# Top-k attention with two expert layers on one core: ten instead of eight slots of the fullest expert start in the attention phase

## The chip, the cores and the metric

The kernel runs on one core of one Trainium2 chip. The metric is the device time of one execution in microseconds. Three runs of the kernel before gave 954.03, 956.29 and 954.28 us; their median is 954.28 us.

## What is computed

Three layers follow each other; every tensor is float32.

1. Attention over 4 batches, 8 heads, 576 positions and head size 64. Of each row of scores only those that reach its 32nd largest value stay; softmax, then the product with v.
2. A dense layer on the 2304 tokens (512 wide): `h = max(x@w1, x@w2, x@w3)` (768 wide), then `h @ w_out`.
3. Routing: each token goes to the expert (one of 8) with the largest logit; `relu(x @ w1[e]) @ w2[e]` (1024 wide inside), scaled by the softmax weight of that expert.

```python
logits = x @ w_gate; expert_idx = np.argmax(logits, axis=1)
...
h = np.maximum(xe @ w1[e], 0.0)
out[mask] = gate_w[mask, None] * (h @ w2[e])
```

With the inputs that the reference draws, the reference's own arithmetic routes 2122 of the 2304 tokens to one expert. In the order in which the kernel ranks its 18 tiles of 128 tokens, that expert has 1051 tokens after nine tiles, 1170 after ten and 1286 after eleven.

## The kernel before, in words

The attention is cut into 144 tiles (128 query rows of one head; the last 64 rows of two heads share one). One Python loop writes out the whole program, one step (`t`, in the code also `clock[0]`) after another. In each step it issues the stages of several tiles (scores, top-k rounds on VectorE, masking, exp, the transposed probabilities, the product with v 14 steps after the scores are worked on), and then fills TensorE with units of the later layers. The order of the instructions on every engine and queue is thus fixed when the program is written; no engine chooses.

**Jobs.** One tile of 128 tokens whose attention is done becomes a job: six `unit_h` (L355, 36 matmuls of 128 columns), two `unit_x2` (L1170 to L1172, 9 matmuls of 512 columns), `unit_gate` (L1192 to L1194) and `unit_rank` (L1236, L1237). After the rank, a row of counts (`snap`) is kept, and the tile's rows are scattered to a DRAM buffer `xs` by expert (L1257, an indirect DMA of GpSimd). The tile then counts as ranked. The last job is tile 15.

**Slots.** The expert that has most tokens after two ranked tiles is picked. A slot is 128 rows of it. `open_slots` opens slot number n as soon as n+2 tiles are ranked and the slot before is open. A slot opened before step 140, and while fewer than `NS1` slots exist, is early, otherwise late; there are at most ten (`NSL`), and late ones open only after step 160.

- An *early* slot does its first layer in two visits, one for each half of the expert's first weight matrix (1024 columns in two halves of 512). Only one half is on the chip at a time, in `W1h` (`half_piece`: four loads of 256 KB, each split into a high and a low float16 part). Each visit loads the slot's rows turned (`xTe`), runs two `unit_e1` (24 matmuls of 128 columns each, L355), and writes the relu, also in two parts, to a DRAM buffer `hs` (L1432). The halves are swapped when every begun visit is done and enough slots wait for the other half: four while the step is under 140 and fewer than `NS1` slots exist, else one. When both halves of a slot are done, its hidden rows are loaded back, 512 KB, into one of two buffers `hTe` (L1385), and four `unit_e2` (L366 to L368, six matmuls of 512 columns each) do its second layer.
- A *late* slot needs the whole first matrix `W1e`, which is loaded in steps 161 to 168. Four `unit_late` (L355, tile `W1e`) do its first layer, and its hidden rows stay on the chip (L1410, L1411) in buffers of their own (three); then come the same four `unit_e2`.

**What sets the order.** `run_units` works with credit: each step adds 1.4 (1.8 once the second matrix is on the chip, 2.0 after step 160), up to 1.2 (2.5 after step 160); units are issued while it is above zero. A `unit_h` or `unit_x2` costs 1.0, a gate 0.25, a rank 0.05, any expert unit 0.67. First come visits of early slots, then jobs, then late slots' first layers, then second layers. A new job may start 2 steps after it is made, its first `unit_x2` 3 steps after its last `unit_h`, its gate 4 steps after the second `unit_x2`, its rank 2 steps after the gate; it is ranked 2 steps after that. A visit starts 2 steps after its rows are loaded and is done 3 steps after it ran. A second layer starts 2 steps after its `hTe` load is issued, and that load is issued once fewer than two early slots hold one. At most four PSUM tiles are live.

```python
early = picked and picked + 8 < clock[0] < TSTOP and len(slots) < NS1
...
if todo[half[0]]:
    ...
elif all(len(s.begun) == len(s.done) for s in slots if not s.late) and len(todo[1 - half[0]]) >= (NSWAP if clock[0] < TSTOP and len(slots) < NS1 else 1):
    half[0] = 1 - half[0]
```

In the program before, slots 0 to 7 are early and open in steps 59, 62, 67, 78, 88, 98, 105 and 110; tile 8 is the tenth ranked tile (step 122) and tile 9 the eleventh (step 129). Visits: half 0 for slots 0 to 3, half 1 for slots 0 to 7 (the last in step 120), a swap in step 123, and half 0 for slots 4 to 7 in steps 136, 139, 142 and 145. Slots 8 and 9 are late: their first layers are the units of steps 170 and 172. The last job is made in step 160; its two `unit_x2` are issued in step 167, its gate in 171, its rank in 173. Second layers: slots 0 to 5 before that rank, slots 6 to 9 behind it.

**The last stage.** `load_ahead` loads the raw weights of a second expert (eight loads of 512 KB, L1347, steps 168 to 175). When all 18 tiles are ranked, `finale` writes the last stage: zero rows behind each expert's rows in `xs` (L340, on the queues of SyncE and ScalarE), a table of what is left to do (some 60 small VectorE instructions, L268 to L331), then loads of weights (L439, L448) and rows (L423 to L428). Then seven dense tiles of the fullest expert (weights `W1e`) alternate with seven half tiles of the others.

Names in the profile: `mm<-xTe,W1h` is a first layer of an early slot, `mm<-xTe,W1e` of a late one, `mm<-…,hTe` a second layer, `ph<-W1h,W1e` the first layer of a dense tile of the last stage (its rows lie in `W1h`), and L1237 the second matmul of a rank.

Of the kernel before, what the change touches and what calls it, by code (L numbers as in the profile page):

```python
# [19 lines left out]
def kernel(  # L20
# [35 lines left out]
    DOWN = 2.0 ** -68  # L56
    LOW = -1.0e30
    UNIT_RATE, TAIL_RATE = 1.08, 2.0
    NEARLY, NPICK, NMIX, NS1 = 10, 2, 7, 8
    CAP, XA, NSL, NLD, NAHEAD = 1.2, 3, 10, 4, 4  # L60
    NSWAP, XLAG, KLAG, TSTOP, EARLY_RATE, LATE_RATE = 4, 2, 2, 140, 1.4, 1.8
    RANK_LAG = 1
# [1695 lines left out]
```

## Time and profile before

| | us |
|---|---|
| median of three runs | 954.28 |
| the profiled execution | 951.46 |
| its span, first to last instruction | 949.7 |
| TensorE busy | 751.6 |
| VectorE busy | 762.5 |
| ScalarE busy | 694.3 |
| GpSimd busy | 608.6 |
| mean granted TensorE clock, share of full speed | 0.96 |

The profile shows one execution; the time of that execution is 1.76 us longer than its span and 2.82 us under the median of the three runs. Busy shares are means over stages. In the fortieths of the span VectorE stands at 9 tenths or more through nearly all of the first 27 (some 640 us), TensorE from about there to nearly the end.

### The profile page before, as it was taken

The page shows a single profiled execution, that of the slowest core. Times are in us where ns is not written, and L with a number is a line of the kernel's source. Part 1 is how long each engine was busy: PE and PEld are TensorE (multiplying, and loading weights), DVE is VectorE, ACT ScalarE, POOL GpSimd, SP SyncE. Part 2 cuts the span into 40 slices and gives each one's busy share as a digit, 9 for nine tenths or more (in the row PEclk, how much of TensorE's full clock was granted, in tenths as well). Part 3 has the DMA queues.
Part 4 walks back from the last instruction along what each step waited for, and adds up shares of the span by engine and source line. Part 5 has one row for each costly group of instructions (what it writes and reads, how often), then busy time and mean ns, then how long its engine had stood idle before and what let it go on. Part 6 is the DMA issues. An engine that isn't in the chain of part 4 may idle for free. (4 is left out here: it accounts for less than half of the span.)

```text
span 949.7 us, 29065 instructions
## 1 busy us (share of the span) xinstructions
PE 751.6 (79%) x10606; PEld 578.1 (61%) x10606; DVE 762.5 (80%) x3110; ACT 694.3 (73%) x1463; POOL 608.6 (64%) x552
## 2 busy tenths in 40 slices
PE   0212368888777899878898998889999999999992
PEld 0100237666555677657677787567887767588881
DVE  4999999999998999998998899788972335567671
ACT  2668899997898988898897997887863231466661
POOL 1457798998988789787877898687985221111110
PEclk9999999999998999899989999889999999999996
DMA  9681977775996788699969888687799358699270
GB/s 229 204 260 29 223 158 153 138 143 105 184 165 151 143 161 175 111 206 176 173 128 179 170 139 154 131 188 127 170 168 156 91 150 278 177 299 279 63 216 16
DMA packets 372164, 155.93 MB, mean 164 GB/s; under 512 B 331931, under 2 KB 348319, under 8 KB 372000
## 3 DMA queue, kind: packets, MB, share of 16 engines
q1 hardware_dynamic: 368128, 143.10, 71.9%
q0 software_dynamic: 3136, 9.46, 2.8%
q8 instruction: 87, 1.43, 0.6%
q10 hardware_dynamic: 736, 1.32, 0.5%
q14 instruction: 77, 0.63, 0.3%
HBM read 76.06 MB, written 16.67 MB: 98 GB/s over the span
## 5 line engine op out<-in xcount | busy, mean ns | idle before, releaser
L355 PEld LDWEIGHTS <-W 128*128 128x128 f16 x4560 | 248.2, 100 | 28.0 <-issue 25.2
L965 POOL TENSOR_TENSOR f<-s,g 128x576 f32<-128x576 f32 x144 | 200.9, 1395 | 69.6 <-DVE vec L974 32.9
L355 PE MATMUL mm<-xT,W 128*128 128x128 f16 x3456 | 210.5, 222 | 18.2 <-DVE W1h L741 6.8
L1058 POOL TENSOR_TENSOR phl<-e,phl 128x576 f16<-128x576 f32 x144 | 186.3, 1293 | 8.1 <-ACT phl L1054 7.9
L913 DVE MAX8 c<-s 128x8 f32<-128x96 f32 x864 | 175.2, 243 | 8.3 <-ACT s L899 4.7
L892 PEld LDWEIGHTS <-qT 128*128 128x128 f16 (+1 forms) x640 | 56.3, 108 | 188.9 <-issue 156.6
L892 PE MATMUL S<-kt,qT 128*128 128x64 f16 (+3 forms) x320 | 62.4, 345 | 109.9 <-ACT s L899 94.4
L1077 PE MATMUL av<-vh,pt 128*128 128x65 f16 (+3 forms) x1600 | 112.4, 201 | 17.4 <-DVE xn L1126 12.9
L1043 ACT ACTIVATE e<-s,be 128x576 f32<-128x576 f32 x144 | 110.6, 768 | 7.7 <-POOL phl L1058 5.7
L974 DVE MAX8 vec<-f 128x8 f32<-128x576 f32 x144 | 108.8, 755 | 5.3 <-POOL f L965 1.4
L959 ACT ACTIVATE g<-s,bf 128x576 uint16<-128x576 f32 x144 | 111.1, 771 | 0.1
L1048 DVE SCALAR_TENSOR_TENSOR e<-s,hkth,e 128x576 f32<-128x576 f32 x72 | 104.1, 1446 | 8.3 <-ACT e L1043 8.1
L1077 PEld LDWEIGHTS <-pt 128*128 128x128 f16 (+3 forms) x2400 | 90.8, 104 | 30.5 <-issue 17.6
L1054 ACT ACTIVATE phl<-e 128x576 f16<-128x576 f32 x144 | 97.4, 676 | 11.3 <-DMA pt<-phl 11.3
L899 ACT ACTIVATE s<-S 128x576 f32<-128x576 f32 x144 | 92.3, 641 | 15.5 <-PE S L892 14.6
L1077 PE MATMUL av<-vl,pt 128*128 128x64 f16 (+3 forms) x800 | 101.6, 199 | 0.0
L1037 POOL TENSOR_TENSOR s<-s,g 128x576 f32<-128x576 f32 x72 | 95.9, 1331 | 0.3
L456 DVE SCALAR_TENSOR_TENSOR W<-st,W 128x1024 f16<-128x1024 f32 x56 | 65.8, 1220 | 36.7 <-ACT W L455 34.6
L892 PE MATMUL S<-kT,qT 128*128 128x512 f16 (+3 forms) x320 | 48.5, 293 | 18.7 <-ACT s L899 18.7
L455 ACT ACTIVATE W<-st 128x1024 f16<-128x1024 f32 x56 | 55.6, 1046 | 1.8 <-DMA st<-in_moe_w_dram 1.8
L1034 ACT ACTIVATE g<-s,hkth 128x576 uint16<-128x576 f32 x72 | 55.4, 769 | 0.0
L1161 POOL TENSOR_TENSOR hhl<-a,hhl 128x384 f16<-128x384 f32 x36 | 34.7, 964 | 28.9 <-ACT hhl L1160 28.9
(232 smaller groups left out, 1586.4 us busy)
## 6 DMA issues: line engine op xcount, KB each, us to landing
st<-in_moe_w_dram SPq DMA_DIRECT2D x72, 512.0 KB
st<-in_moe_w_dram SPq DMA_DIRECT2D x28, 256.0 KB
raw<-in_moe_w_dram SPq DMA_DIRECT2D x12, 512.0 KB
st<-in_v_dram SPq DMA_DIRECT2D x16, 256.0 KB
hs<-he SPq DMA_DIRECT2D x16, 256.0 KB
hTe<-hs SPq DMA_DIRECT2D x8, 512.0 KB
st<-in_q_dram SPq DMA_DIRECT2D x15, 256.0 KB
qT<-qT SPq DMA_DIRECT2D x30, 128.0 KB
```

The costliest lines, as they stand in the source:

```text
L355: nc.tensor.matmul(out=ps[:, o * n:(o + 1) * n], lhsT=w(b, kk, c), rhs=x(a, kk), start=(kk == 0 and i == 0), stop=(kk == KD - 1 and i == 2))
L892: nc.tensor.matmul(out=ps[o:o + m, j, 0:(REM if j else NQ * P)], lhsT=qt[:, vv, hh, 0:m], rhs=kr[:, hh] if j else km[:, hh // HG, :, hh % HG],
L913: nc.vector.max(out=c[:, i * 8:(i + 1) * 8], in_=s[:, i * CW:(i + 1) * CW])
L959: nc.scalar.activation(out=gg[n], in_=Ss[n], func=ACTF.Sign, bias=bf[g][:, i], accum_out=cnt[g][:, i])
L965: nc.gpsimd.tensor_tensor(out=ff[n], in0=Ss[n], in1=gg.pop(n).bitcast(F16), op=ALU.subtract)
L974: bulk.append(lambda: nc.vector.max(out=y8[g][:, i, 1:9], in_=y))
L1037: nc.gpsimd.tensor_tensor(out=Ss[n], in0=Ss[n], in1=zz.pop(n).bitcast(F16), op=ALU.subtract)
L1043: nc.scalar.activation(out=e, in_=Ss.pop(n) if early(n) else Ss[n], func=ACTF.Exp, scale=ESC, bias=be[g][:, i])
L1048: nc.vector.scalar_tensor_tensor(out=e, in0=Ss.pop(n), scalar=kth[g][:, i:i + 1], in1=e, op0=ALU.is_ge, op1=ALU.mult)
L1054: nc.scalar.activation(out=ph[:, 0, 0:S], in_=p, func=ACTF.Copy)
L1058: nc.gpsimd.tensor_tensor(out=ph[:, 1, 0:S], in0=p, in1=ph[:, 0, 0:S], op=ALU.subtract)
L1077: nc.tensor.matmul(out=av[o:o + m, i, 0:n], lhsT=t[0:kk, p * NCH + c, o:o + m], rhs=v_rows(x, b, c, hh)[:, 0:n], start=(c == 0 and p == 0 ...
```

## The change

One constant: `NS1`, the number of slots that may be early, goes from 8 to 10.

```diff
-    NEARLY, NPICK, NMIX, NS1 = 10, 2, 7, 8
+    NEARLY, NPICK, NMIX, NS1 = 10, 2, 7, 10
```

So the ninth and the tenth slot (8 and 9) open when ten and eleven tiles are ranked, and their first layers are done in two visits each, with the half weights, as those of the other eight. No late slot is left. The total of ten slots, their rows, and the last stage's tiles stay as they are.

## Rows read from the trace of the kernel before

**Rows 1.** The page, busy time of engines: busy us, share of span, instructions.

```profile
PE 751.6 (79%) x10606; PEld 578.1 (61%) x10606; DVE 762.5 (80%) x3110; ACT 694.3 (73%) x1463; POOL 608.6 (64%) x552
```

**Rows 2.** Stretches: us, busy of PE, PEld, DVE, ACT, POOL; clock, DMA share, GB/s.

```profile
700.00:760.00 60.00, 59.74 (x812) 45.46 (x809) 22.03 (x86) 21.19 (x41) 28.63 (x34) 1.00 0.65 126
760.00:800.00 40.00, 39.87 (x442) 27.92 (x439) 14.91 (x56) 12.28 (x25) 7.16 (x9) 1.00 0.66 196
...
796.40:817.30 20.90, 20.86 (x100) 9.38 (x98) 15.18 (x72) 6.91 (x9) 3.13 (x4) 1.00 0.73 267
817.30:819.40 2.10, 0.07 (x2) 0.07 (x2) 2.10 (x3) 2.10 (x3) 1.62 (x1) 1.00 0.63 125
819.40:935.70 116.30, 113.29 (x1848) 91.20 (x1847) 72.40 (x79) 67.84 (x86) 14.21 (x15) 1.00 0.71 194
```

**Rows 3.** Groups by line, whole span: first layers of early, then late slots.

```profile
L355 PE MATMUL mm<-xTe,W1h 128*128 128x128 f16 x768 | 48.5, 224 | 1.1 <-DVE xr L1178 0.8 <-DMA xTe<-xs 0.3
...
L355 PE MATMUL mm<-xTe,W1e 128*128 128x128 f16 x192 | 11.1, 219 | 0.1
```

**Rows 4.** Timeline of TensorE, 785 to 825 us: start, us, what, idle before.

```profile
785.02 5.52 PE L355 MATMUL mm<-xTe,W1e 128*128 128x128 f16 x96
...
790.96 5.53 PE L355 MATMUL mm<-xTe,W1e 128*128 128x128 f16 x96
...
796.36 0.17 PE L1237 MATMUL mm<-oh,ones 128*128 128x8 f16 x1
...
816.88 0.38 PE L368 MATMUL mm<-vh,hTe 128*128 128x512 f16 x1
819.33 5.52 PE L355 MATMUL ph<-W1h,W1e 128*128 128x128 f16 x96 [2.06 <-DMA W1h<-xs]
```

**Rows 5.** Groups of TensorE from 796.4 to 817.3 us; one of six alike.

```profile
L366 PE MATMUL mm<-kt,hTe 128*128 128x512 f16 x16 | 6.1, 379 | 0.0
```

**Rows 6.** Timeline of VectorE behind the last rank.

```profile
796.57 0.17 DVE L1264 TENSOR_TENSOR vec<-mm,base 128x8 f32<-128x8 f32 x1 [1.34 <-PE mm L1237]
...
797.16 0.69 DVE L1411 SCALAR_TENSOR_TENSOR hTe<-mm,hTe 128x512 f16<-128x512 f32 x1
...
809.27 0.18 DVE L331 TENSOR_TENSOR chg<-new,live 1x31 int32<-1x31 f32 x1
```

**Rows 7.** Timelines of GpSimd (first row) and of SyncE's queue, same stretch.

```profile
798.98 0.99 POOL L1257 DMA_INDIRECT xs<-xr,si  x1 [9.74 <-DVE lv L270]
...
805.36 4.40 SPq L340 DMA_DIRECT2D xs<-zrow  x4
812.18 1.26 SPq L439 DMA_DIRECT2D st<-in_moe_w_dram  x4
...
816.14 1.30 SPq L427 DMA_TRANSPOSE W1h<-xs  x1
```

**Rows 8.** DMAs: loads of hidden rows, SyncE's wait for their buffer (700 to 800 us), all scatters.

```profile
hTe<-hs SPq DMA_DIRECT2D x8, 512.0 KB
...
SPq L1385 <- PE mm L368: 7.7, 2, 6.0
...
DMA to landing us min/median/max: 3.3/4.3/6.3
```

**Rows 9.** Stretches as in rows 2: a TensorE gap, then three times 3 us.

```profile
378.90:383.50 4.60, 0.04 (x1) 0.00 (x0) 4.50 (x7) 0.70 (x3) 3.12 (x4) 0.82 0.41 91
383.59:386.59 3.00, 3.00 (x22) 1.67 (x22) 2.93 (x19) 2.51 (x6) 1.16 (x1) 0.50 0.02 5
386.59:389.59 3.00, 3.00 (x14) 1.15 (x12) 2.88 (x18) 3.00 (x7) 1.65 (x3) 0.65 0.49 90
389.59:392.59 3.00, 3.00 (x61) 2.89 (x60) 2.94 (x15) 3.00 (x9) 2.89 (x3) 1.00 0.86 194
```

**Rows 10.** Splitting of half weights on VectorE, whole span, and a gap of 1.7 us.

```profile
L741 DVE TENSOR_TENSOR W1h<-mm,W1h 128x512 f16<-128x512 f32 x11 | 7.6, 691 | 10.9 <-ACT mm L740 10.7
...
697.66 0.18 PE L1236 MATMUL mm<-oh,tri 128*128 128x8 f16 x1 [1.70 <-DVE oh L1226]
```

## The prediction

> **What bounds the kernel now.** The busy times of the engines come first: TensorE and VectorE are both near 80% [rows 1], so the stage decides. The stretches of the end show which: from 700 us on TensorE is busy 59.74 of 60 us and then 39.87 of 40 at clock 1.00, while VectorE stands at 22.03 of 60 and 14.91 of 40 [rows 2]. The last stage, 819.4 to 935.7 us, is TensorE's too (113.29 of 116.3). The order of TensorE's work shows the joint: the first layers of slots 8 and 9 run at 785.0 and 791.0 us, the last rank ends at 796.5, then second layers run until 817.26, then TensorE is idle for 2.06 us until the last stage's rows have landed at 819.33 [rows 4]. So two things compete to set when the last stage starts: the work that TensorE still has, and the chain behind the last rank. The chain wins by 2.06 us today. Its links: the rank's counts on VectorE, the scatter issued at 798.98, the zero rows issued at 805.36 when it has landed, the table done at 809.45, weight loads at 812.18, the load of rows at 816.14 [rows 6, 7]. From rank to first matmul it takes 819.33 - 796.36 = 23.0 us.
>
> **What the change moves.** Slots 8 and 9 open at ten and eleven ranked tiles, steps 122 and 129, both under 140. The tokens of the expert are then 1170 and 1286, over the 1152 and 1280 that nine and ten full slots need, so both are full and the last stage's list stays the same. The swap in step 123 comes as before: slot 8 is not open yet, and four slots wait. Half 0 then serves slots 4 to 9: the new visits run in steps 148 and 151, right behind slot 7's in 145. In step 154 the halves are swapped a third time (after step 140 one waiting slot is enough), the four pieces of half 1 are loaded again in 155 to 158, and the other visits run in 163 and 166.
>
> *First layers on TensorE.* Removed: 192 matmuls, 11.1 us [rows 3]. Added: 192 of the same form; at the mean of the early ones, 48.5/768 x 192, they take 12.1 us, but that mean holds stretches of low clock, and here the clock is 1.00 [rows 2]. I take 11.4, so +0.3 (bounds 0 and +1.0). Old and new place lie in the same solid stretch: steps 148 to 166 are about 703 to 770 us, and TensorE idles 0.26 us between 700 and 760. **Nothing is saved by the move itself.**
>
> *The order.* This is the term that counts. Following the credits by hand: the visit in 148 delays tile 12's second `unit_x2` to 149, the one in 151 sends slot 1's second layer to 153 and 159 (before: 151, 152) and slot 2's to 160, 166, 167. The two visits after 160 go ahead of the jobs, so the last `unit_h` of tile 15 slips from step 164 to 165, its `unit_x2` from 167 to 168, its gate from 171 to 172 and its rank from 173 to 174. Before, the late slots' units filled steps 170 and 172 and kept second layers out (in 171 three PSUM tiles were taken). Now second layers fill them: slot 4 in 170, slot 5 in 172, three units of slot 6 in 173. So 27 second-layer units stand ahead of the last rank where 24 stood, and 13 behind it where 16 stood. Sixteen take 817.26 - 796.38 = 20.9 us [rows 4]; their matmuls are 96, six groups of 16 [rows 5]; one unit is 1.3 us. All first layers are ahead of the rank in both programs. Hence the rank comes 3 x 1.3 = **3.9 us later** on TensorE, and only 13 x 1.3 = 17 us of work are left to cover its chain. If my count is off by a step, the shift is 0 or about 8 us; these are its bounds.
>
> *The chain.* One instruction goes out of it: the 0.69 us split of slot 9's hidden rows at 797.16, L1411 [rows 6]: -0.6. An earlier scatter gains little: it took 6.4 us where the median is 4.3 [rows 7, 8], but the table ends only 0.3 us before the zero rows are issued (809.45 against 809.76), so -0.3 is the bound. New ahead of it on SyncE's queue: the loads of the hidden rows of slots 8 and 9, which wait for a buffer that the second layer two slots earlier frees. The last of them waits for the end of slot 7, 1.3 + 5.2 = 6.5 us behind the rank; the zero rows waited until 8.9 us behind it (805.36 - 796.5), so it is hidden; without that cover it costs what slot 7 is late. ScalarE's half of the zero rows stands behind slot 7's output in the same way, with about 1.7 us of cover left.
>
> *The clock.* TensorE's idle time ahead of the last stage grows to 2.1 + 3.9 - 0.6 = 5.4 us. The gap of 2.07 us today and one of 1.7 us leave the clock at 1.00 [rows 2, 10]. A gap of 4.6 us does not: the next 3 us run at 0.50, the 1.2 GHz level, the 3 us after them at 0.65, then 1.00 [rows 9]. Lost are 0.50 x 3 + 0.35 x 3 = 2.5 us of full speed work, here in a stage that TensorE bounds. Bounds 0 and 2.6; I take 2.5, the gap being nearer to that row.
>
> *What costs nothing.* The half weights again: four splits of 0.69 us on VectorE [rows 10] and eight copies of 0.6 on ScalarE, in a stretch where both are idle for over half the time [rows 2]. DMA: 1 MB of weights, 1 MB out to `hs`, 1 MB back, at a DMA share of 0.65. The loads of hidden rows pace the second layers, as only two buffers serve slots 4 to 9: one is free when a slot ends, and TensorE has the next slot, 5.2 us, to cover the load. 512 KB [rows 8] at the 267 GB/s of the densest stretch [rows 2] take 2.0 us, and a load of rows needed 1.9 us from the end of its issue to its use (819.33 - 817.44), so 3.9 us are hidden in 5.2. With one raw weight load ahead of it, 5.9 us: 0.7 us shows for each of the two slots ahead of the rank. Bounds 0 and 4; I take 0, since SyncE waited for such a buffer for 7.7 us in all and TensorE never waited for a load [rows 8, 2].
>
> **The sum**: +0.3 + 3.9 - 0.6 + 2.5 = +6.1 us. Against the profiled execution, 951.46 us, that is 957.6; the median of the runs lies 2.82 us above that execution, so **960.4 us**, +0.6%. About 0.3%, 2.9 us, is what a measurement can tell from no change.
>
> **Rivals.**
>
> *Faster: TensorE has room.* The weight loads of TensorE, PEld, are busy 45.46 of 60 us and 27.92 of 40 [rows 2], so 26.6 us look free between 700 and 800 us, more than the 11.1 us that move. If the visits ran in that room, the rank and the work behind it would come 11.1 us earlier: 943.2 us. It decides if TensorE is truly idle where the visits are put. Against it: 96 matmuls of 512 columns in 20.9 us are 0.217 us each, and 512 columns at 2.4 GHz are 0.213; with 512 columns per load of weights a low PEld is no room. Idle time that could be filled is 0.4 us in the hundred, and the 1.7 and 2.06 us gaps [rows 10, 4], at most about 4 us (950). I give it 0.06. The Trainium skill, Perfetto Trace Analysis, section Identifying the Most-Contended Engine, says that matmul busy time is no good measure and that headroom is judged by the busy share of weight loads and by the floating-point rate; by the first the move would pay, and the rows here speak for the second.
>
> *The same.* No second layer gets ahead of the rank, because a load or a PSUM tile holds slot 6 back: +0.3 - 0.6, 954 us. Or one or two units do and the gap stays short enough for the full clock: 1.3 x 2 - 0.3 = +2.3, 956.6. For it: the margin is one step of a plan counted by hand. I give it 0.24.
>
> *Slower still: loads of hidden rows show.* Eight raw loads share SyncE's queue with them and each waits behind a buffer; if the two slots ahead of the rank and the zero rows each slip 1 to 2 us, 3 to 5 us are added: 964. Chance 0.11.
>
> *It does not do what it says.* If the count were under 1280 at step 129, a slot would be blank and its 128 rows would go to the end: a dense tile there is 5.5 + 4 x 1.3 = 10.7 us, with serial loads before it, 966 or more. The margin is 6 tokens. Chance 0.02.
>
> **The numbers.** Forecast 0.57. Slower by over 0.3%: 0.57 + 0.11 + 0.02 = 0.70; the same 0.24; faster 0.06. The range goes from 952.5, which takes in most of the same, to 966, the loads that show; within the likeliest case alone, the clock's cost at 0 and a little of the loads give 957.9 (960.4 - 2.5) to 963.
>
> **What would show it.** Right: late first layers (`mm<-xTe,W1e`) gone, 16 rows of half-weight splits, a last rank near 800 us (796.4 + 3.9 + 0.3), 13 units behind it, some 5 us of idle TensorE waiting for the rows of `W1h`, and a clock near 0.5 right after. The last stage starts near 823 us (819.3 + 3.9 + 0.3 - 0.6) and takes 2 to 3 us longer than 116.3. Wrong: a rank at 796 or earlier, no longer gap, or waits of TensorE on `hTe`; and a last stage that starts before 817 us would refute the reading that TensorE has no room.

## The result, and the profile after

Four runs of the changed kernel gave 965.0 to 970.81 us, median 968.21; four of the kernel before on the same chip gave a median of 954.15. The ratio is **1.0133** (95% interval 1.0095 to 1.0171): slower by about 13 us (14 by the medians), where +6 was forecast. The sign is right, the size is not, and 968.21 lies above the range (966.0). The profiled execution took 965.0 us. Executions over 1.5% above the fastest of their kernel are left out of the figures of this document; that is one, of 980.49 us, in the second measurement of the changed kernel.

The first layers moved as described. The group of early first layers has 960 matmuls instead of 768 [rows 3], the late form is gone, and the group costs 59.3 - 48.5 = 10.8 us more where 11.1 went. The group of the changed kernel, then its list of DMAs (28 loads of 256 KB and 8 of hidden rows stood there before):

```profile
L355 PE MATMUL mm<-xTe,W1h 128*128 128x128 f16 x960 | 59.3, 222 | 1.6 <-DVE xr L1178 0.8 <-DMA xTe<-xs 0.7
```

```profile
st<-in_moe_w_dram SPq DMA_DIRECT2D x32, 256.0 KB
...
hTe<-hs SPq DMA_DIRECT2D x10, 512.0 KB
```

The joint to the last stage looks different from [rows 4]. Timeline of TensorE of the changed kernel:

```profile
799.20 0.17 PE L1237 MATMUL mm<-oh,ones 128*128 128x8 f16 x1
...
814.70 0.38 PE L368 MATMUL mm<-vh,hTe 128*128 128x512 f16 x1
826.56 0.61 PE L366 MATMUL mm<-kt,hTe 128*128 128x512 f16 x1 [11.48 <-DMA hTe<-hs]
...
833.79 0.89 PE L355 MATMUL ph<-W1h,W1e 128*128 128x128 f16 x13
```

The rank comes at 799.2 instead of 796.4, but the last stage starts at 833.8 instead of 819.3: from the start of the rank to the stage it takes 34.6 us instead of 23.0. In between TensorE runs the second layers of slots 6, 7 and 8, then stands for 11.48 us, and what it waits for is not the rows of the last stage but the hidden rows of slot 9. The stretches say what that does to the clock (columns as in [rows 2]):

```profile
700.00:760.00 60.00, 58.60 (x843) 46.33 (x841) 23.66 (x73) 24.81 (x49) 27.97 (x33) 1.00 0.73 152
...
815.00:826.50 11.50, 0.07 (x1) 0.00 (x0) 5.32 (x5) 7.67 (x9) 2.03 (x2) 0.74 0.78 247
826.50:829.50 3.00, 2.94 (x7) 1.04 (x8) 3.00 (x4) 1.27 (x2) 0.00 (x0) 0.50 0.71 124
829.50:832.50 3.00, 3.00 (x12) 1.23 (x11) 0.85 (x1) 0.00 (x0) 0.00 (x0) 0.79 0.38 66
...
833.80:950.00 116.20, 113.36 (x1849) 91.27 (x1847) 69.19 (x76) 66.73 (x84) 15.87 (x15) 1.00 0.73 188
```

Slot 9's 24 matmuls take from 826.56 to the end of the last one at 833.96, 7.4 us, where a slot took 20.9 / 4 = 5.2 [rows 4]: 2.2 us are the clock's, at 0.50 and then 0.79. The last stage itself then runs at 1.00 and is no longer than before.

Why slot 9's hidden rows are late stands in SyncE's queue. Its timeline in the changed kernel:

```profile
793.89 0.33 SPq L1385 DMA_DIRECT2D hTe<-hs  x1
...
804.75 0.34 SPq L1385 DMA_DIRECT2D hTe<-hs  x1
...
813.24 4.36 SPq L340 DMA_DIRECT2D xs<-zrow  x4
819.97 1.26 SPq L439 DMA_DIRECT2D st<-in_moe_w_dram  x4
821.51 1.18 SPq L448 DMA_DIRECT2D st<-in_moe_w_dram  x4
822.79 0.34 SPq L1385 DMA_DIRECT2D hTe<-hs  x1
823.88 1.30 SPq L427 DMA_TRANSPOSE W1h<-xs  x1
```

The load at 793.89 is slot 6's, the one at 804.75 slot 8's. Slot 9's is issued at 822.79, behind the four issues of zero rows and eight weight loads of the last stage; its buffer had been free since slot 7 ended, about 810. And the zero rows are themselves late: at 813.24, 14.0 us behind the rank, where they were issued at 805.36, 9.0 behind it [rows 7]. They wait for the last tile's scatter, on GpSimd's queue. First the last output ahead of that scatter in the kernel before, then the changed kernel:

```profile
788.06 0.98 POOL L400 DMA_INDIRECT out_dram<-ye,mte  x1 [4.62 <-DMA out_dram<-ye,mte]
```

```profile
795.71 0.97 POOL L400 DMA_INDIRECT out_dram<-ye,mte  x1 [5.07 <-DMA out_dram<-ye,mte]
...
802.07 0.98 POOL L400 DMA_INDIRECT out_dram<-ye,mte  x1 [5.19 <-DMA out_dram<-ye,mte]
808.33 0.97 POOL L400 DMA_INDIRECT out_dram<-ye,mte  x1 [5.28 <-DVE cnt L323]
809.61 0.97 POOL L1257 DMA_INDIRECT xs<-xr,si  x1 [0.30 <-issue]
```

The scatter (L1257) was issued 2.6 us behind the rank before [rows 4, 7]; now 10.4 behind it: the outputs of slots 5 and 6 (L400, at 802.07 and 808.33) stand ahead of it in GpSimd's queue, each issued some 6.3 us after the one ahead. The rows at 795.71 and 802.07 show the wait for the output ahead to land; at 808.33 the profile names another wait, with the same spacing. Before, slot 5's output stood at 788.06, ten us ahead of the scatter, as the late slots' first layers (785 to 796 us, [rows 4]) lay between it and the rank.

### The profile page after: what moved, and what is told of

Read it like the earlier page. It is cut to its first block, busy times and chain, and to the rows that moved or that the text cites. A ratio compares the mean times of both kernels' runs of the same rounds, so it can differ in the third digit from the quotient of the medians.

```text
span 963.3 us, 29131 instructions
## 1 busy us (share of the span) xinstructions
PE 752.9 (78%) x10606; PEld 579.6 (60%) x10606; DVE 765.6 (79%) x3114; ACT 697.2 (72%) x1467; POOL 610.0 (63%) x552
## 5 line engine op out<-in xcount | busy, mean ns | idle before, releaser
L355 PEld LDWEIGHTS <-W 128*128 128x128 f16 x4560 | 252.6, 101 | 31.4 <-issue 28.5
L355 PE MATMUL mm<-xT,W 128*128 128x128 f16 x3456 | 215.0, 224 | 19.1 <-DVE W1h L741 5.9
L1077 PE MATMUL av<-vh,pt 128*128 128x65 f16 (+3 forms) x1600 | 110.3, 200 | 14.3 <-DVE xn L1126 10.3
L1048 DVE SCALAR_TENSOR_TENSOR e<-s,hkth,e 128x576 f32<-128x576 f32 x72 | 103.3, 1435 | 9.1 <-ACT e L1043 8.9
L1054 ACT ACTIVATE phl<-e 128x576 f16<-128x576 f32 x144 | 97.5, 677 | 10.4 <-DMA pt<-phl 10.4
L355 PE MATMUL mm<-xTe,W1h 128*128 128x128 f16 x960 | 59.3, 222 | 1.6 <-DVE xr L1178 0.8
L355 PEld LDWEIGHTS <-W1h 128*128 128x128 f16 x960 | 55.1, 99 | 2.9 <-issue 1.0
```

What stands on the lines that cost most here:

```text
L355: nc.tensor.matmul(out=ps[:, o * n:(o + 1) * n], lhsT=w(b, kk, c), rhs=x(a, kk), start=(kk == 0 and i == 0), stop=(kk == KD - 1 and i == 2))
L1048: nc.vector.scalar_tensor_tensor(out=e, in0=Ss.pop(n), scalar=kth[g][:, i:i + 1], in1=e, op0=ALU.is_ge, op1=ALU.mult)
L1054: nc.scalar.activation(out=ph[:, 0, 0:S], in_=p, func=ACTF.Copy)
L1077: nc.tensor.matmul(out=av[o:o + m, i, 0:n], lhsT=t[0:kk, p * NCH + c, o:o + m], rhs=v_rows(x, b, c, hh)[:, 0:n], start=(c == 0 and p == 0 ...
```

## The experiments

All ratios are to the kernel before, run on the same chip and beside it; the chip differs from group to group, so medians of different groups are not set against each other. For the reading across profiles one table is used. Its columns are worked out from timelines: the start of the 122nd tile's exponential (up to there the programs differ in little more than the place of the scatter and the opening of slot 8, some 35 us ahead of it), and from there the time to the last product with v, to the end of the last rank, to the first matmul of the last stage ("the chain" below), and to the end of the span.

| profile | 122nd tile | to last av | to rank | to stage | to end |
|---|---|---|---|---|---|
| before | 623.5 | 116.3 | 56.7 | 22.8 | 130.4 |
| before, second profile | 629.5 | 115.3 | 57.0 | 23.4 | 133.2 |
| after | 625.1 | 118.6 | 55.7 | 34.4 | 129.5 |
| after, second profile | 628.9 | 121.3 | 55.7 | 34.3 | 130.9 |
| load first | 628.8 | 119.1 | 55.7 | 29.4 | 132.4 |
| no outputs | 625.6 | 119.1 | 55.7 | 31.9 | 131.1 |
| both | 629.6 | 118.5 | 55.7 | 26.5 | 133.4 |
| before, only the traffic | 627.2 | 116.6 | 57.2 | 25.5 | 131.2 |
| nine early slots | 625.2 | 118.0 | 60.9 | 24.8 | 134.8 |
| mended, full output | 626.9 | 122.7 | 55.7 | 27.5 | 133.0 |
| mended, three buffers | 627.5 | 124.7 | 53.1 | 26.1 | 135.2 |
| before, scatter later | 608.4 | 118.0 | 57.7 | 24.6 | 133.1 |
| after, scatter later | 612.3 | 120.7 | 55.7 | 34.6 | 132.3 |
| mended, scatter later | 607.2 | 125.4 | 53.1 | 27.2 | 132.0 |

**Slot 9's load first.** The last stage's instructions are written only when every slot's load of hidden rows has been issued.

```diff
-  lambda: all(s.open for s in slots),
+  lambda: all(s.open and (s.late or s.hT is not None) for s in slots),
```

> Edit: the changed kernel, but the last stage is written only once the hidden rows of all early slots have been asked for, so slot 9's load stands ahead of the table, the zero rows and the weight loads on SyncE's queue. Theory A (that load was issued at 822.8 us instead of about 809.8, behind everything that waits for the table): the 11.5 us wait of TensorE for it goes, slot 9's second layer ends near 820, and the last stage starts when its rows land, near 826 instead of 833.8: about 960.4 us (968.2 - 7.8). Theory B (GpSimd issues the last scatter 10.2 us behind the rank instead of 2.6) is untouched by this: the zero rows stay near rank + 14. Theory C (more DMA and splitting work in the same stretch, no order): no change, 966 to 971.

966.18 us (five runs, 962.65 to 967.21), ratio 1.0085 (1.0053 to 1.0117). SyncE's queue and TensorE's only long gap near the stage, then two stretches, of this kernel:

```profile
813.95 0.34 SPq L1385 DMA_DIRECT2D hTe<-hs  x1
819.55 4.32 SPq L340 DMA_DIRECT2D xs<-zrow  x4
```

```profile
832.96 1.33 PE L355 MATMUL ph<-W1h,W1e 128*128 128x128 f16 x11 [8.68 <-DMA W1h<-xs]
```

```profile
833.00:836.00 3.00, 3.00 (x29) 3.00 (x29) 3.00 (x4) 1.70 (x2) 0.00 (x1) 0.50 0.52 137
836.00:839.00 3.00, 3.00 (x43) 3.00 (x42) 1.06 (x2) 0.60 (x1) 0.00 (x0) 0.74 0.48 88
```

The wait for hidden rows is gone and the chain is 5.0 us shorter (34.4 to 29.4): the queue order was a cause. But the chain is still 6 us longer than in the kernel before, the rows of the last stage are now what comes last, and the low clock only moves into the stage. The time came down less than to the 960 that this theory alone wants.

**No outputs of slots 5 and 6.** Their rows of the output are computed but not scattered, so this kernel leaves part of the output out.

```diff
+  if s.i in (5, 6):
+      nc.scalar.activation(out=y, in_=ps, func=ACTF.Copy, scale=mte[:, s.i, 0:1])
+  else:
+      put_y(ps, mte[:, s.i], y)
```

> Edit: the changed kernel, but the output scatters of slots 5 and 6, which stand ahead of the last tile's scatter on GpSimd's queue, are left out (those rows of the output are not written). Theory B: the last scatter is issued near rank + 3 instead of rank + 10.2, the zero rows go out some 5 us earlier, and with them the weight loads, slot 9's load and the rows; the wait of TensorE for slot 9 shrinks from 11.5 to about 7 us and the time falls by 4 to 5 us, to about 963.9. Theory A alone: slot 9's load still stands behind the table's loads, so most of the wait stays. Theory C: no change beyond 1 us.

966.7 us (965.15 to 975.57), ratio 1.0138 (1.0079 to 1.0198). GpSimd's scatter, 3.05 us behind the rank at 800.21, and TensorE's gap:

```profile
803.26 0.98 POOL L1257 DMA_INDIRECT xs<-xr,si  x1 [5.00 <-issue]
```

```profile
824.77 0.61 PE L366 MATMUL mm<-kt,hTe 128*128 128x512 f16 x1 [8.84 <-DMA hTe<-hs]
```

The scatter is back in its place and the zero rows come at 8.95 us behind the rank, as before; the chain shortens by 2.5 us only, since slot 9's load still stands behind the last stage's instructions. In the time no difference to the unedited change can be seen (1.0138 beside 1.0133).

**Both edits at once** (the output of slots 5 and 6 left out here too).

> Edit: the two edits above together. A and B together: the last stage starts near 823 us instead of 833.8, so about 957.6 us (968.2 - 10.6), 3 to 4 us over the kernel before; TensorE's gap ahead of the last stage is 2 to 4 us. If A and B each cost what they should and nothing else does, what is left against the kernel before is the rank that comes 2.8 us later. Theory C: 966 or more.

963.19 us (962.64 to 969.4), ratio 1.008 (1.0049 to 1.0111). From rank to stage 26.5 us, a gap of 5.65. So the two queues explain 34.4 - 26.5 = 7.9 of the 11.6 us by which the chain grew (34.4 - 22.8). Most of the rest seems to be the load of hidden rows itself, which now stands *ahead* of the zero rows on SyncE and waits for slot 7 until 10.7 us behind the rank, so that the zero rows go out at 11.9 instead of 9.0; that is read from the order of the queue. And 0.8% were left where the theory wanted less: the gap of 5.65 us brings the clock down in the stage (0.50 in its first 3 us, 0.69 in the next 3).

**Only the traffic.** The kernel before, with the traffic of the change and none of its work: the half weights loaded once more in steps 155 to 158, four writes to `hs` and two copies of 512 KB.

```diff
+  if not general and 155 <= t <= 158:
+      half[0] = 1
+      pend_w.append(half_piece(t - 155))
```

> Edit: the kernel before (two late slots), to which the added transport is added without its order: half 1 of the weights loaded and split once more in steps 155 to 158 (not used), four writes of 256 KB to the DRAM buffer at the steps of the new visits, and two copies of 512 KB inside DRAM at the steps of the two new loads of hidden rows. Theory C: this alone costs most of the 14 us, 962 to 968. Theories A and B: within 2 us of the kernel before, 954 to 956.

959.21 us (ten runs, 954.76 to 963.03), ratio 1.0024 (1.0001 to 1.0047): the traffic and the four splits are worth some 2 us, 4.5 at most by the interval. But the chain is 25.5 us, 2 to 3 longer than in the two profiles of the kernel before (22.8, 23.4), with a gap of 4.76 us. The zero rows go out as early as before; from them to the load of rows (L340 to L427) SyncE's queue takes 13.4 us (809.79 to 823.19) instead of 10.8 (805.36 to 816.14, [rows 7]).

**The kernel before again**, for a second profile and for the spread.

> The kernel before once more, for a second profile of it beside those of this call. In the profiles so far the attention phase ends between 739.8 and 748.1 us, which hides shifts of a few us; what is compared is the time from the last rank to the first matmul of the last stage, 23.0 us before, 34.6 after. Every theory: 23.0 within 1 us again, ratio 1.00.

957.32 us (ten runs, 954.16 to 961.8), ratio 0.9997 (0.9975 to 1.0019). Its profile is 8.7 us longer than the first, 6.0 of them at the 122nd tile: executions of one and the same kernel drift apart in the attention. The chain is the same (23.4 us).

**Nine early slots.** One constant: `NS1` is 9, so only slot 8 moves.

> Edit: NS1 = 9, so only one of the two slots moves. In this plan all loads of hidden rows stand ahead of the last stage's instructions, and the late slot 9 keeps its own buffer; 28 units of second layers stand ahead of the last rank (24 before), and the output scatters of slots 5 and 6 stand right ahead of the last tile's scatter. Theory B and the plan: no wait of TensorE for hidden rows; the last scatter is issued near rank + 6 to 10, the zero rows near rank + 12 to 14, the last stage starts 26 to 30 us behind the rank, and the rank itself is 5 us later: 960 to 965 us. If the cost simply went with the number of slots moved, it would be half of that of the changed kernel, near 961, with half of its wait for hidden rows (5 to 6 us).

966.99 us (965.01 to 969.25), ratio 1.0098 (1.0061 to 1.0134). One slot costs nearly as much as two, 2 us more than the expected 960 to 965. The chain is nearly the old one (24.8 us, where 26 to 30 were expected), with the scatter issued 3.4 us behind the rank, but here the fault that was forecast for ten slots does come: 28 units of second layers stand ahead of the rank, which comes 60.9 us behind the attention's end instead of 57, and 12 units don't cover the chain (the clock is 0.50 and 0.60 in the first two stretches of 3 us behind this gap):

```profile
828.91 1.33 PE L355 MATMUL ph<-W1h,W1e 128*128 128x128 f16 x11 [9.21 <-DMA W1h<-xs]
```

**Mended, with the full output.** Slot 9's load first, and the outputs of slots 5 and 6 kept back until the last scatter is issued.

```diff
+  put_y(ps, mte[:, s.i], y, held if clock[0] >= 173 and len(ranked) < NTT else None)
...
   ranked.append(j)
+  if len(ranked) == NTT:
+      for go in held:
+          go()
```

> Edit: the changed kernel with the last stage written only after all hidden rows are asked for, and with the output scatters of slots 5 and 6 held back until the last tile's scatter is issued (nothing left out). Theories A and B: like the run with both edits, 26 to 27 us from the last rank to the last stage, near 962; what remains over 23.0 is SyncE's queue, which holds the zero rows back behind slot 9's load, as that waits for the end of slot 7's second layer, 10.6 us behind the rank. If the left-out output itself was what saved time, it stays near 966.

967.43 us (961.33 to 972.37), ratio 1.0096 (1.006 to 1.0132), though the chain is 27.5 us. That misses the expected 962 and is no better than the version that left the outputs out. By the time alone the rival of the expectation, that the output left out was itself what saved time, is not excluded; by the chain (27.5 beside 26.5) holding the outputs back does what leaving them out does. This profile also has a long masking at 652.9 us (see below) and 122.7 us to the last product with v.

**Mended, three buffers.** Three buffers `hTe` instead of two (the load no longer waits for slot 7), the outputs held, and a bound on the second layers ahead of the rank, which gives 22 units ahead and 18 behind.

```diff
-  if sum(...) < (2 if e1 else 1):
+  if sum(...) < (3 if e1 else 1):
...
+  ahead_of = 20 if any(j.u <= NU1 + 2 for j in jobs) else 22 if jobs else 99
+  if len(slots) == NSL and 4 * s.i + s.u - 4 >= ahead_of:
+      continue
```

> Edit: the changed kernel with three buffers for hidden rows instead of two, the output scatters of slots 5 and 6 held back as above, and second layers held so that 22 units stand ahead of the last rank and 18 behind it. Theories A and B plus the queue: no load of hidden rows waits long on SyncE's queue, the zero rows go out near rank + 9, the last stage starts 23 us behind the rank and TensorE has 18 x 1.3 = 23.5 us to fill that, so no gap: 2 us less than the kernel before, ratio 0.998, and 14 to 16 us less than the changed one. Theory C (the added transport itself costs): still 5 us or more over the kernel before.

965.93 us (twelve runs, 959.46 to 969.14), ratio 1.007 (1.0041 to 1.0099). The expectation was missed. The chain is 26.1 us: the zero rows go out at 9.2 us behind the rank, as in the kernel before, but from them to the load of rows it takes 13.0 us (814.36 to 827.33) instead of 10.8, as in the run with only the traffic. The gap is 2.81 us, and still 7 us stay. The table shows where: 124.7 us from the 122nd tile to the last product with v, 8 to 9 more than the kernel before. So the largest difference of this kernel lies **in the attention**, ahead of everything that had been looked at; 3.6 us of it come back on the way to the rank, where two units fewer stand. The timeline of VectorE of this kernel has the largest single instruction there:

```profile
653.55 6.90 DVE L1053 SCALAR_TENSOR_TENSOR e<-s,hkth,e 128x576 f32<-128x576 f32 x1
```

A masking (L1048 in the unedited kernels) that takes 0.81 us when it is not held up took 6.9. Such long ones stand in the kernel before too, elsewhere. One of them on VectorE and what GpSimd does meanwhile, kernel before:

```profile
375.72 6.92 DVE L1048 SCALAR_TENSOR_TENSOR e<-s,hkth,e 128x576 f32<-128x576 f32 x1
```

```profile
375.39 1.01 POOL L1257 DMA_INDIRECT xs<-xr,si  x1 [0.15 <-issue]
376.43 1.30 POOL L1037 TENSOR_TENSOR s<-s,g 128x576 f32<-128x576 f32 x1
377.66 1.29 POOL L965 TENSOR_TENSOR f<-s,g 128x576 f32<-128x576 f32 x1
378.90 1.28 POOL L1058 TENSOR_TENSOR phl<-e,phl 128x576 f16<-128x576 f32 x1
380.13 0.67 POOL L1099 TENSOR_TENSOR xhl<-xn,xhl 128x256 f16<-128x256 f32 x1
380.75 1.27 POOL L1037 TENSOR_TENSOR s<-s,g 128x576 f32<-128x576 f32 x1
```

The masking begins 0.33 us after the scatter and ends 0.6 us after GpSimd's row of back-to-back instructions. Where a masking begins during one of GpSimd's subtractions, it usually waits for the end of that one instruction (in 40 of 44 such cases of this profile), and GpSimd's next one comes out half a us longer. The next three runs move the scatter.

**The scatter later.** A tile's scatter is issued behind GpSimd's next subtraction, in the kernel before, in the changed one, and in the mended one.

```diff
-  nc.gpsimd.indirect_dma_start(out=xs, ...)
+  late_put.append(lambda: nc.gpsimd.indirect_dma_start(out=xs, ...))
...
       st_drop(n)
+  for go in late_put:
+      go()
+  late_put.clear()
```

> The kernel before with one edit: a tile's scatter is issued behind GpSimd's next subtraction of the same step (about 1.3 us later) instead of ahead of it. In all ten profiles so far four maskings on VectorE (at about 215, 376, 470 and 582 us) take 4.6 to 7.1 us instead of 0.8: each begins 0.3 to 0.9 us after such a scatter has begun and ends only when GpSimd's row of back-to-back instructions ends. If it is the scatter under way at the masking's start that locks VectorE out, the four long maskings go (20 us of VectorE) and the time falls by 8 to 20 us, to about 0.985. Rival: any back-to-back row of GpSimd does it, wherever the scatter stands; then as many long maskings appear elsewhere and the time stays within 0.4%.

> The changed kernel with the same edit of the scatter's place. If the change's cost is the late start of the last stage (11 to 12 us behind the rank) and 2 to 3 us at the end of the attention, it stays 12 us, 1.2%, above the kernel before with that edit. If a good part of the cost is maskings locked out in some executions (one near 652 us of 6.9 us stood in three of the seven profiles with ten or nine early slots and in none of three with eight), the difference to it is under 8 us.

> The mended version of the change (three buffers of hidden rows, outputs of slots 5 and 6 held behind the last scatter, 22 second-layer units ahead of the rank) with the same edit of the scatter's place. It came 7.7 us above the kernel before, and its profile had one masking of 6.9 us at 653 us that no profile of the kernel before has. If that lock was half of it, it comes within 4 us of the kernel before with the same edit. If not, 7 to 8 us above it again.

> The changed kernel once more, unedited. The theory (two queues make the last stage late: slot 9's load of hidden rows behind SyncE's last-stage instructions, outputs of slots 5 and 6 ahead of the last tile's scatter on GpSimd): from the last rank to the last stage's first matmul 34 us again (34.6 the first time, 23.0 and 23.5 in two profiles of the kernel before), an idle stretch of TensorE of 9 us or more that ends with slot 9's load, the last tile's scatter some 10 us behind the rank; ratio 1.009 to 1.017. Rival (the first profile was a rare execution): the chain is under 28 us and the ratio under 1.007.

Beside these four the kernel before took 954.18 us (23 runs).

- The kernel before with that edit: **943.94 us** (940.7 to 950.59), ratio **0.9899** (0.9858 to 0.994). It beats both kernels, and the fall of 10 us lies in the expected 8 to 20. The group of maskings, of the kernel before and of this one:

```profile
L1048 DVE SCALAR_TENSOR_TENSOR e<-s,hkth,e 128x576 f32<-128x576 f32 x72 | 104.1, 1446 | 8.3 <-ACT e L1043 8.1
```

```profile
L1048 DVE SCALAR_TENSOR_TENSOR e<-s,hkth,e 128x576 f32<-128x576 f32 x72 | 87.8, 1220 | 9.2 <-ACT e L1043 9.1
```

The four long maskings behind a scatter are gone; one at 677 us (4.85 us), where no scatter stands, is not. (The expectation says that all ten profiles had the four; the one with nine early slots had three of them.) The edit has a price as well: the last tile's scatter now stands behind an output on GpSimd's queue, 7.7 us behind the rank instead of 2.6, and the chain is 24.6 us instead of 22.8.

- The changed kernel with that edit: 955.59 us (951.05 to 959.9), ratio 1.001 (0.9986 to 1.0033). That is 11.65 us more than the run above, as expected: **without the maskings held up behind a scatter the change still costs 1.2%**.
- The mended one with it: 949.63 us (945.45 to 954.48), ratio 0.9944 (0.9917 to 0.9971), 5.7 us above the first. Less than 4 was expected if the masking near 653 us was half of what the mended version lost, 7 to 8 if it was not; it came out between. The comparison is blurred, as the edit undoes a part of the mending: the last scatter is issued 10.3 us behind the rank instead of 2.0, and the zero rows at 13.6 instead of 9.2. And that masking is not what makes this kernel's attention long: the time to the last product with v, where the long masking stood, did not shrink without it: 125.4 us beside 124.7. What TensorE loses there is idle time (11.6 us beside 7.5 in the kernel before with the same edit; the longest waits are 2.55 and 3.16 us) and clock (a mean of 0.95 beside 0.97). Why the mended version has these was not tried.
- The changed kernel, unedited, again: 972.74 us (five runs, 965.78 to 976.25), ratio 1.0177 (1.0134 to 1.0221), a little over the 1.009 to 1.017 expected. The chain is the same to 0.1 us, and the wait too:

```profile
832.86 0.61 PE L366 MATMUL mm<-kt,hTe 128*128 128x512 f16 x1 [11.41 <-DMA hTe<-hs]
```

Behind the 122nd tile this execution had one long masking that the first profile of it had not, behind the scatter at 653 us (6.92 us); its "to last av" is 2.7 us longer, for which this masking is the likely cause.

What is left in the attention without long maskings is 120.7 against 118.0. When the changed and the unchanged kernel with the late scatter are laid side by side from the 120th tile on, the changed one has the opening of slot 9 there, six small instructions of VectorE. These are the first of the six, the masking among them, and the wait of TensorE behind them (changed kernel, scatter later):

```profile
613.34 0.13 DVE L229 TENSOR_TENSOR m8s<-snap,vec 1x8 f32<-1x8 f32 x1
...
616.13 1.69 DVE L1048 SCALAR_TENSOR_TENSOR e<-s,hkth,e 128x576 f32<-128x576 f32 x1
```

```profile
619.67 5.58 PE L355 MATMUL mm<-xR,W 128*128 128x128 f16 x72 [2.54 <-DVE ls L1221]
```

Counted from the split ahead of them (L741, 612.40 and 608.50 in the two kernels), that masking begins 0.47 us later, takes 1.69 us instead of 0.81, and TensorE waits 2.54 us instead of 1.46 for the gate's VectorE step. In the kernel before these two slots open at 757 and 762 us, behind the attention. But the delay does not last: at the 126th to 128th tile's exponential the two kernels are level again. They part by 2.6 us up to the 131st, and on that way TensorE waits, in the changed kernel alone, for the rows of a visit that both kernels have:

```profile
645.30 1.97 PE L355 MATMUL mm<-xTe,W1h 128*128 128x128 f16 x27 [1.94 <-DMA xTe<-xs]
```

The two unedited kernels, in their first profiles, have no such wait; they are level at the 141st tile's exponential, 84.2 us behind the 122nd in both, and part at the last two tiles. There the visits of steps 148 and 151 stand, and with them a wait that all nine profiles with ten early slots have (1.1 to 1.6 us) and none of the four with eight (changed kernel, unedited):

```profile
740.96 2.17 PE L355 MATMUL mm<-xT,W 128*128 128x128 f16 x36 [1.40 <-DVE base L1265]
```

A later last product is not all loss, though: the new visits put work of TensorE ahead of it that stood behind it before, and the way from there to the rank is 1.0 us shorter. Up to the end of the rank TensorE is busy for 166.8 us in the changed kernel and 167.1 in the kernel before, and the rank comes 1.3 us later. That the visits cause this was not tried alone.

## Why the forecast was right in sign and wrong in size

*"Nothing is saved by the move itself"*: right. 10.8 us were added where 11.1 went, -0.3 where the term was +0.3, and the rival of free room on TensorE did not come.

*"27 second-layer units stand ahead of the last rank … and 13 behind it"*, +3.9: wrong, and the smaller of the two steps that failed. Visits, swap, gate and rank stand in the steps that the prediction names. But the program has slot 4's second layer as three units in step 170, where the step's credit ends, and the fourth in 171; so slot 6's hidden rows, which wait for that slot's buffer, are asked for in step 172 (SyncE's row at 793.89, right behind the end of slot 4's second layer at 793.7), and slot 6 may start in step 174, the rank's own, where the plan counted on 173. So 24 units stand ahead and 16 behind, as before; the shift by this term was the lower bound, 0. The rank is 2.8 us later in the first profile, but 1.6 of that stood at the 122nd tile already; from there on it is 118.6 + 55.7 = 174.3 us against 116.3 + 56.7 = 173.0. So the rank near 800 us that was named as a sign of being right did come (799.2), but not by this term. With nine early slots 28 units did stand ahead: the mechanism exists, in the other kernel.

*"The chain. One instruction goes out of it"*, -0.6: wrong, and **this is the step that failed**, since it carries the miss: the chain grew by 11.6 us (22.8 to 34.4). Two parts of it were wrong.

- *"The last of them waits for the end of slot 7, … 6.5 us behind the rank; … so it is hidden"*. With three more units behind the rank than counted, slot 7 ends one step later, in step 176, where the last stage's instructions begin to be written; the load is issued in step 177, behind them on SyncE. It cost what the prediction says it costs without its cover: TensorE waits 11.48 us for it. Issued first it takes 5.0 us off the chain.
- GpSimd's queue was not walked through: the late first layers that went had kept the outputs of slots 5 and 6 away from the last scatter. It came 7.8 us later, the zero rows 5.0; leaving the two outputs out takes 2.5 us off the chain alone, and 2.9 with the load first (29.4 to 26.5).

With nine early slots, where 28 units are ahead, neither happened (scatter 3.4 us behind the rank, no wait for hidden rows, a chain of 24.8). That points to the wrong count as the root of both; no run with ten slots shows it.

*The clock, 2.5*: right in size, 2.2 us, but partly by luck: it was lost in slot 9's second layer, behind a gap of 11.48 us instead of 5.4, and not in the last stage. Where a gap of about the forecast size did stand ahead of the last stage (5.65 us, both edits), the clock was 0.50 and then 0.69 in the stage, close to the 0.50 and 0.65 of [rows 9]. *"The loads of hidden rows … I take 0"*: the bound of 4 was meant for SyncE's raw loads and a late buffer; the place in the queue was not among its cases. *"Wrong: … waits of TensorE on `hTe`"* was named as the sign of a failure, and it is the row that showed it. The rival of 964 by loads that show had the right object, at a third of its size. So the sign came out right, but by way of terms that the prediction held at nothing: that is luck as well.

*What costs nothing* held only in part: the traffic alone costs some 2 us (1.0024) and lengthens the chain by 2 to 3.

*What is not in the sum at all*: the wait of 1.1 to 1.6 us at the end of the attention, and a long masking that appears in some executions (at about 653 us in four of the ten profiles with nine or ten early slots, in none of the four with eight).

Together, by the two profiles with the late scatter, where no long masking confuses it behind the 122nd tile (another one, at 282 us, where the programs do not differ yet, sets the changed kernel back by some 4 us ahead of it): +2.7 to the last product, -2.0 to the rank, +10.0 in the chain, -0.8 in the stage, about +9.8 us; the medians say 11.65. By the first pair: +2.3, -1.0, +11.6 and -0.9. Of the chain's growth in the first pair, 11.6 us, the two queues are 7.9 (shown). Of the other 3.7, 2.9 are the zero rows that wait behind slot 9's load when it goes first (argued from its place in the queue). With three buffers they no longer wait (9.2 us behind the rank), and the chain is still 26.1; 2.2 of these 3.3 us are the longer way from the zero rows to the load of rows, which the run with only the traffic has too. That points to the added traffic, but no run takes it away alone.

## What to carry to other kernels

Taking work out of a late stretch also takes away what kept other things apart in it: before moving it, write down for each in-order queue (the DMA queues and GpSimd's too) which instruction now stands directly ahead of the one that the critical chain begins with. A load that is "hidden" has a place in a queue as well as a time, and one step of the plan can put it behind the whole next stage. And when two profiles of the same kernel differ in a stretch that the change does not touch, look for single instructions that are many times their usual length: here the four in the kernel before were worth 1.0%, nearly as much as the change cost.

## What the runs showed of the hardware that was not expected

- VectorE can be kept waiting by GpSimd for several instructions on end. When a masking began 0.33 to 0.56 us after an indirect DMA had started on GpSimd, it took 4.9 to 7.1 us instead of 0.81 and ended 0.62 us behind GpSimd's row of back-to-back instructions; this holds for all 40 such cases in the 14 profiles. Of the other maskings that began during such a DMA, the five that began within its first 0.23 us took 0.81 us (for example at 507.04 us in the second profile of the kernel before, the scatter at 506.81), all seven that began 0.86 us into it took 4.6, and of seven in between five took 0.81 and two 3.4 and 4.7. Begun during a subtraction a masking mostly waits for that one instruction (for example 0.81 + 0.88 = 1.69 us). The Trainium skill, SBUF — State Buffer, section SBUF: two separate sides, says that the two engines share a pair of ports as an exclusive lock that is held for the whole instruction. The usual waits agree with that; the long ones, over four to six instructions of GpSimd, go beyond one instruction, and the measurement decides. Why the port is not handed over then was not settled: a few long maskings (at about 285, 546 and 692 us, 4.5 to 6.2 us, not all in every profile) have no scatter in front of them.
- These waits stand at fixed places in most executions and come or go at a few others with a start that differs by a few tenths of a us. They are 4 to 6 us each, as large as the drift of 6 us between two profiles of the same kernel; the second profile of the kernel before has one at 547 us (4.68 us) that the first has not.
- Output scatters on GpSimd's queue follow each other at 6.3 us in this program (795.71, 802.07, 808.33), and whatever stands behind them waits with them.
